# Values of the first six pairs of heads multiplied in plain float32, and the first token mix at two units per slot

## The chip, the cores and the metric

The kernel runs on one core of a Trainium2 chip. The metric is the device time of one execution in microseconds; lower is better. TensorE (PE) multiplies, VectorE (DVE), ScalarE (ACT) and GpSimd (POOL) work on what it leaves, and the queue of SyncE (SP) starts the transfers.

## What is computed

Decay attention over 8 batches of 8 heads (576 tokens, head size 64), and then a token mix of low rank and a feed-forward layer, all in float32:

```python
scores = q @ k.T / sqrt(D) + cum[:, None] - cum[None, :]   # cum: cumulative log of f, causal
attn = softmax(scores)
x = concat_heads(attn @ v)                                 # [8, 576, 512]
u = x + (x.T @ U @ V).T                                    # U, V of rank 32
out = u + relu(u @ w_ch1) @ w_ch2                          # 512 -> 2048 -> 512
```

The weights arrive as 64-bit floats and are decoded on the chip.

## The kernel before

**Split operands.** A product in float32r takes one array pass but keeps fewer bits of its operands. So the kernel splits an operand into a high part (`h`, a rounding copy on ACT) and a low part (`l`, the rest, a subtraction on DVE or POOL) and adds several products. For the values, `make_vs` lays the high and the low part of V side by side in the 128 columns of the stationary operand `VS`, one arrangement per head; `evac` brings the transposed probabilities from PSUM as `PTh` (ACT, line 380) and `PTl` (DVE, line 381); `values` multiplies `VS` with `PTh` and then with `PTl` (lines 462 and 465), so that the two halves of the result `pv` hold the products with high V and with low V. ACT copies one half out (`cr`, line 473) and DVE adds the other (`xT`, line 474).

**Steps and slots.** The program goes through 32 pairs of heads. Step `p` has ten slots `s`. In step `p` PE scores pair `p` (head 0 in slots 0 to 3, the tails of both heads in 4 and 5, head 1 in 6 to 9), transposes the probabilities of pair `p-1` (`T`, `T_v`), multiplies the values of pair `p-1`, head 0 (slot 7) and of pair `p-2`, head 1 (slot 0), transposes the results (`Tx`, `Ty`) and projects them on the rank (`ranks`, `Tt`). PE's order is the order of the code. That of DVE, ACT and POOL is set by a scheduler, and in steps 1 to 6 that of SP's queue too. `defer` and `at` write the work of the other engines into later slots.

**Operands of the scores.** `split_qk` makes the parts of q and k (`HL`), and `place` copies them by DMA into `G[0]` and `G[1]`, one per head of a pair, each a single buffer: the next pair's parts can go there when the last score of this head is done.

**Decodes.** Fourteen weight blocks are decoded by `decode` (four operations on DVE, lines 61 to 64, three on POOL, one on ACT). Two come at the start, and the table `DECODES` gives step and slot of the other twelve, the last six of which are blocks of the second weight matrix.

**Fillers.** After the fourth pair of a batch has gone through, ten mix units of that batch (five `hmix`, five transposes `tu`, `tv`) are taken one per slot of a step; for the first batch this is step 6. Then its feed-forward units (24 or 27 per batch, `A` of twelve 256-column products, `B` of six 512-column products) fill slots 1 to 6, 8 and 9 of the next steps. Four are held back for the slots of the next mix. Mix units and feed-forward units share the two PSUM banks of the pool `psF`. The stores of the mixed tokens to DRAM (`ud`) follow the last mix unit.

**After step 33** a second sweep goes over the rest of the hidden features, batch by batch.

Of the kernel before, what the change touches and what calls it, by code (L numbers as in the profile page):

```python
# [8 lines left out]
F32 = mybir.dt.float32  # L9
F32R = mybir.dt.float32r  # L10
# [7 lines left out]
B, H, S, D = 8, 8, 576, 64  # L18
# [15 lines left out]
PTW = 1536  # L34
NG = B + 1
NX = 3


@with_exitstack
def tile_decay_attention_moe(ctx, tc, qk, v, f, U, V, w1, w2, out):  # L40
# [9 lines left out]
    def decode(raw, a, h, l, eng, rows=slice(0, 128), keep=False):  # L50
        """float64 words (low, high) of `raw` [.., 2] as float32 in two parts h + l [..]; `a`
        is int32 scratch, and so is `raw` in the end. Read as a float32, the high word has the
        sign and the upper bits of the exponent in the right place: a product changes the bias.
        `eng`: the engine for a part that several can do; `rows`: where the low part is wanted;
        `keep`: not before what `eng` has been given so far."""
        lo, hi = raw[..., 0].bitcast(U32), raw[..., 1]
        af, gf = a.bitcast(F32), hi.bitcast(F32)
        first = eng.tensor_scalar(af, gf, 2.0**-112, None, op0=ALU.mult)
        if keep:
            tc.keep_in_program_order(first)  # L60
        nc.vector.tensor_scalar(hi, hi, -0x80000000, None, op0=ALU.bitwise_and)
        nc.vector.scalar_tensor_tensor(a, a, 3, hi, op0=ALU.logical_shift_left, op1=ALU.bitwise_or)
        nc.vector.tensor_scalar(hi, a, -0x800000, None, op0=ALU.bitwise_and)
        nc.vector.scalar_tensor_tensor(gf, lo, 2.0**-52, gf, op0=ALU.mult, op1=ALU.mult)
        nc.gpsimd.tensor_tensor(af, af, gf, op=ALU.add)
        nc.scalar.copy(h, af)
        nc.gpsimd.tensor_tensor(l[rows], af[rows], h.bitcast(F32)[rows], op=ALU.subtract)
# [23 lines left out]

# [1 line left out]
    DG, ZR = 384, 512  # L93
    HW = S // 2
    # Operands of the scores, per head of a pair: planes 0, 1 hold q (stationary), 2, 3 hold k.
    # Columns: head 0 [main 512 | tail 64 | zeros 64], head 1 [zeros 64 | tail 64 | main 512]
    # (k of head 1 keeps its order).
    G = [att.tile([P, 4, 640], F32R, name=f"G{j}") for j in range(2)]
# [30 lines left out]

# [1 line left out]
    def decay_log():  # L131
# [24 lines left out]

# [1 line left out]
    w1h = wt.tile([P, NA, NDC, P], F32R, name="w1h")  # L158
# [3 lines left out]
    Us = wt.tile([P, NM + 1, 2 * RK], F32R, name="Us")  # L162
    VV = wt.tile([P, S], F32R, name="VV")  # rows: the high part three times, the low part once

# [12 lines left out]

    # The decodes, in order: each takes its turn in the tiles that the first sweep uses later.
    UNITS = [("w1", 0), ("w1", 1), ("U", 0), ("w1", 2), ("w1", 3), ("V", 0), ("w1", 4), ("w1", 5)]
# [3 lines left out]
    def load_w(u):  # L183
# [4 lines left out]
        if kind == "w2":  # L188
            # The last buffer of X has no use before batch 2.
            spare = xn[NX - 1].rearrange("p c d -> p (c d)").bitcast(I32)  # L190
            if fc % 2:
                raw, a = spare[:, 1536:2560], sb.tile([P, 512], I32, tag="w2a", name=f"stg{u}")
            else:
                raw, a = spare[:, 0:1024], spare[:, 1024:1536]
        else:
            t = sf.tile([P, 3 * S], I32, tag=("uh", "ul", "hh")[u % 3], name=f"stg{u}")
            raw, a = t[:, 0 : 2 * n], t[:, 2 * n : 3 * n]
# [32 lines left out]

# [1 line left out]
    st = {}  # L232
    filler = []
    SPARE = (2, 4)
    # Work of the other engines on what TensorE leaves behind, by slot and by phase in the slot.
    later = {}
# [21 lines left out]
    def load_v(p):  # L258
        vr = sb.tile([P, NM + 1, P], F32, tag="vr", name=f"vr{p}")
        st[p]["vr"] = vr.rearrange("p c (j d) -> p c j d", j=2)  # L260
# [3 lines left out]

    def make_vs(p):
        vr = st[p]["vr"]
        VS = sb.tile([P, NM + 1, 2, P], F32R, tag="VS", name=f"VS{p}")
# [7 lines left out]
    def split_qk(p, eng=nc.gpsimd):  # L275
        qk = st[p]["qk"]
        # Until the first sweep starts, one of its tiles serves as a second buffer.
        spare = p in SPARE
# [30 lines left out]
    def bank_s(p, name):  # L309
        """Before the first mix starts, the banks of the fillers serve the scores too."""  # L310
        scored[0] += 1
# [67 lines left out]
    def evac(dsth, dstl, src):  # L379
        defer(0, lambda: nc.scalar.copy(dsth, src))  # L380
        defer(2, lambda: nc.vector.tensor_tensor(dstl, src, dsth.bitcast(F32), op=ALU.subtract))  # L381

    GRP = (((0, 0), (0, 1), (0, 2), (0, 3)), ((1, 1), (1, 2), (1, 3)), ((2, 2), (2, 3), (3, 3)))

    def turn_p(p, j, g):
        z = st[p]
        if "PTh" not in z:
            z["PTh"] = sb.tile([P, 2, PTW], F32R, tag="PTh", name=f"PTh{p}")
# [12 lines left out]
        for c in sorted({c for c, _ in grp}):  # L401
            m = sum(1 for cc, _ in grp if cc == c)
            sl = slice(OC[c], OC[c] + P * m)
            evac(z["PTh"][:, j, sl], z["PTl"][:, j, sl], tp[:, P * x : P * (x + m)])
            x += m

    def turn_tail(p):
# [6 lines left out]
        for c in range(0, NM, 2):  # L414
            o = [(OC[c + y] + MAIN - P * (c + y)) // TAIL for y in range(2)]
            pair = [
                z[n].rearrange("p j (y d) -> p j y d", d=TAIL)[:, :, o[0] : o[1] + 1 : o[1] - o[0]]
                for n in ("PTh", "PTl")
            ]
            evac(pair[0], pair[1], tpv[:, :, c : c + 2])  # L420

    def turn_small(pa, px):
        """The last keys of pair pa's tail rows, and the last tokens of pair px."""
        tq = psT.tile([P, 512], F32, tag="T", name=f"Ty{pa}_{px}")
# [5 lines left out]
        if pa is not None:  # L430
            pt4 = st[pa]["PT4"]
            defer(0, lambda: nc.scalar.copy(pt4[0:64], tq[0:64, 0:P]))
            defer(
                2,
# [17 lines left out]
    X0 = 384  # L452

    def values(p, j):
        z = st[p]
        if j == 0:
# [47 lines left out]
    def ranks(p):  # L504
# [13 lines left out]

        # Rows of TS: the high parts of x Uh and x Ul, the low part of x Uh, its high part again.
        defer(1, lambda: nc.scalar.copy(TS[0:64, fs], tp[0:64, 0:P]))  # L520
# [7 lines left out]

# [1 line left out]
    cur = [None, None]  # L530

    def mix_units(b):
# [3 lines left out]
        def bank(name):  # L536
            # The banks of the scores are free when the last batch is mixed.
            if b == B - 1:
# [46 lines left out]
        if b < B - 1:  # L585
            return h + t
        # The first sweep of the last batch starts as soon as its first half is mixed.
        return h[0:2] + t[0:2] + h[2:] + t[2:]
# [109 lines left out]
    mixing = []  # L698
    DECODES = [(1, 1), (1, 3), (1, 6), (2, 2), (2, 6), (3, 3), (4, 2), (5, 2), (6, 1), (6, 4), (6, 7), (7, 1)]

    def step(p):
# [8 lines left out]
        for s in range(SLOTS if p <= NP else 6 + 2):  # L710
# [17 lines left out]
            if (p, s) in DECODES:  # L728
                u = 2 + DECODES.index((p, s))
                # The last four use a tile of X again, which the scheduler orders as written here.  # L730
                steps = [lambda: load_w(u + 2), lambda: decode_w(u)]
# [40 lines left out]
            if mixing:  # L772
                mixing.pop(0)[1]()
                if filler and (s in (0, 1, 3, 5) or p >= NP):
                    run_filler()
# [23 lines left out]

# [1 line left out]
    pool = pools(right, "right")  # L801
# [7 lines left out]
    def wb_unit(i, r):  # L809
# [4 lines left out]
        else:  # L814
            nc.sync.dma_start(t, w2_src(NA + i))
            h, l = b2h[i], b2l[i]
        # X of batch 5 is done with.
        a = xn[(B - 3) % NX][:, (2 * i + r) % NM].bitcast(I32)
# [22 lines left out]

# [1 line left out]
    pool = pools(left, "left")  # L843
# [9 lines left out]

    # The last batch comes first: its tokens and its partial sums are still on the chip.
    order = [B - 1, *range(B - 2), B, B - 2]
# [53 lines left out]
def _layout(q, k, v, f, moe_U, moe_V, moe_w_ch1, moe_w_ch2):  # L909
    """The inputs in the order the chip loads them: only rearranged, in their own types."""  # L910
    import numpy as np
# [38 lines left out]
```

## Time and profile before

| | |
|---|---|
| median of 3 runs | 1350.56 us (1349.6 to 1354.66) |
| profiled execution, first to last instruction | 1350.8 us |
| PE busy | 1245.0 us (92%) |
| DVE, ACT, POOL busy | 728.5, 559.8, 307.1 us |

The page shows the profiled execution by its span alone; this span stands for its own time. In the page's slices each digit is the busy share of a 33.8 us stretch in tenths. A table of stretches gives for each its length, the busy time of PE, of the weight loads (PEld), of DVE, ACT and POOL with the number of instructions, the clock that TensorE was granted, the busy share of the DMA engines and GB/s. A row of waits says which instruction waited for which, the sum in us, how often, and the longest.

### The profile page before, as it was taken

The page shows a single profiled execution, that of the slowest core. Times are in us where ns is not written, and L with a number is a line of the kernel's source. Part 1 is how long each engine was busy: PE and PEld are TensorE (multiplying, and loading weights), DVE is VectorE, ACT ScalarE, POOL GpSimd, SP SyncE. Part 2 cuts the span into 40 slices and gives each one's busy share as a digit, 9 for nine tenths or more (in the row PEclk, how much of TensorE's full clock was granted, in tenths as well). Part 3 has the DMA queues.
Part 4 walks back from the last instruction along what each step waited for, and adds up shares of the span by engine and source line. Part 5 has one row for each costly group of instructions (what it writes and reads, how often), then busy time and mean ns, then how long its engine had stood idle before and what let it go on. Part 6 is the DMA issues. An engine that isn't in the chain of part 4 may idle for free.

```text
span 1350.8 us, 19334 instructions
## 1 busy us (share of the span) xinstructions
PE 1245.0 (92%) x6912; PEld 1066.2 (79%) x6912; DVE 728.5 (54%) x1796; ACT 559.8 (41%) x1516; POOL 307.1 (23%) x228
## 2 busy tenths in 40 slices
PE   2678898999998998999999988999999999999998
PEld 2567787888887897888888877788888888888887
DVE  6797976767667667667667599621211212112121
ACT  4666766756666666667567322211101111011110
POOL 4675633222232322222131055400000000000000
PEclk9887899999999999999999999999999999999999
DMA  8966765754755656567544254410321303212010
GB/s 211 231 174 153 185 160 129 211 125 124 192 138 139 189 131 174 154 145 205 122 117 134 71 159 139 180 69 0 125 78 48 125 0 125 87 39 94 0 32 32
DMA packets 89431, 167.02 MB, mean 124 GB/s; under 512 B 8776, under 2 KB 33352, under 8 KB 87288
## 3 DMA queue, kind: packets, MB, share of 16 engines
q1 hardware_dynamic: 89336, 165.79, 44.5%
q8 instruction: 55, 0.90, 0.3%
q14 instruction: 40, 0.33, 0.1%
HBM read 73.33 MB, written 35.78 MB: 81 GB/s over the span
## 4 chain that ended last, share of the span: by engine, by line
PE 70%; DMA 10%; DVE 8%; ACT 5%; SPq 3%; issue 3%; POOL 0%; ACTq 0%; DVEq 0%; POOLq 0%
PE O L882 19%; PE Hb L870 18%; PE A L608 8%; DMA G<-HL 8%; PE B L626 6%; PE V L465 4%; PE S L304 3%; PE T L398 3%; PE S L305 2%; ACT HL L281 2%; PE Tt L515 1%; PE St L304 1%; PE St L305 1%; DMA G<-cumd 1%; SPq L289 1%
## 5 line engine op out<-in xcount | busy, mean ns | idle before, releaser
L875 DVE SCALAR_TENSOR_TENSOR bl<-Hb,bh 128x512 fp32r<-128x512 f32 x90 | 62.2, 692 | 377.6 <-ACT bh L874 377.6
L874 ACT ACTIVATE bh<-Hb 128x512 fp32r<-128x512 f32 x90 | 53.9, 599 | 429.3 <-PE Hb L870 429.3
L870 PE MATMUL Hb<-u,b1h 128*128 128x512 f32 x640 | 213.2, 396 | 0.0
L325 DVE CUSTOM_DVE_ANT_0 S<-S,mask 128x128 f32<-128x128 f32 (+3 forms) x256 | 126.3, 495 | 81.2 <-PE S L305 75.4
L333 ACT ACTIVATE P<-S,nm 128x128 f32<-128x128 f32 (+3 forms) x256 | 136.7, 535 | 63.7 <-DVE nm L325 56.5
L304 PE MATMUL S<-G 128*128 128x128 f32 (+3 forms) x256 | 98.4, 384 | 62.9 <-DMA G<-HL 31.2
L882 PE MATMUL O<-b2h,bl 128*128 128x512 f32 x360 | 142.8, 397 | 2.2 <-DVE bl L875 2.2
L870 PEld LDWEIGHTS Hb<-u,b1h 128*128 128x128 f32 x640 | 120.3, 188 | 29.2
L882 PE MATMUL O<-b2h,bh 128*128 128x512 f32 x360 | 142.2, 395 | 0.0
L882 PE MATMUL O<-b2l,bh 128*128 128x512 f32 x360 | 142.2, 395 | 0.0
L608 PE MATMUL A<-uh,w1h 128*128 128x256 f32 (+1 forms) x384 | 122.0, 318 | 5.6 <-DVE xn L636 4.1
L870 PE MATMUL Hb<-u,b1l 128*128 128x512 f32 x320 | 126.5, 395 | 0.0
L273 POOL TENSOR_TENSOR VS<-vr,VS 128x320 fp32r<-128x320 f32 x64 | 55.3, 884 | 299.8 <-PE T L398 211.3
L381 DVE TENSOR_TENSOR PTl<-T,PTh 128x512 fp32r<-128x512 f32 (+1 forms) x192 | 98.2, 532 | 36.2 <-ACT PTh L380 34.3
L304 PEld LDWEIGHTS S<-G 128*128 128x128 f32 x256 | 51.8, 202 | 81.1 <-ACT P L333 31.1
L608 PE MATMUL A<-uh,w1l 128*128 128x256 f32 (+1 forms) x384 | 114.6, 298 | 0.0
L608 PE MATMUL A<-ul,w1h 128*128 128x256 f32 (+1 forms) x384 | 114.4, 298 | 0.0
L626 PE MATMUL B<-w2h,hh 128*128 128x512 f32 x216 | 92.0, 426 | 4.6 <-DVE ost L644 2.5
L398 PE MATMUL T<-ident,P 128*128 128x128 f32 x544 | 92.0, 287 | 1.9 <-DVE xn L443 1.6
L282 POOL TENSOR_TENSOR HL<-qk,HL 128x1152 fp32r<-128x1152 f32 x30 | 79.7, 2656 | 50.9 <-ACT HL L281 46.5
L305 PE MATMUL S<-G 128*128 128x128 f32 (+3 forms) x256 | 86.7, 340 | 2.1 <-DMA G<-cm 2.1
L380 ACT CAST PTh<-T 128x512 fp32r<-128x512 f32 (+1 forms) x192 | 83.0, 462 | 11.3 <-PE T L398 9.4
(168 smaller groups left out, 2758.5 us busy)
## 6 DMA issues: line engine op xcount, KB each, us to landing
G<-HL SPq DMA_DIRECT2D x192, 288.0 KB
qk<-in_qk_dram SPq DMA_DIRECT2D x32, 576.0 KB
u<-ud SPq DMA_DIRECT2D x16, 1024.0 KB
sr<-in_w_dram SPq DMA_DIRECT2D x20, 512.0 KB
vr<-in_v_dram SPq DMA_DIRECT2D x32, 256.0 KB
accd<-ost SPq DMA_DIRECT2D x32, 256.0 KB
xn<-accd SPq DMA_DIRECT2D x8, 1024.0 KB
out_dram<-xn SPq DMA_DIRECT2D x32, 256.0 KB
```

What stands on the lines that cost most here:

```text
L282: eng.tensor_tensor(HL[:, :, 1], qk, HL.bitcast(F32)[:, :, 0], op=ALU.subtract)
L304: nc.tensor.matmul(ps, lhs[0], G[j][:, 2, cols], start=first, stop=False)
L305: nc.tensor.matmul(ps, lhs[1], G[j][:, 3, cols], start=False, stop=last)
L325: nc.vector.tensor_tensor_reduce(ps[:, :w], ps[:, :w], mask[:, 512 - w : 512], scale=-SCALE, scalar=3.0e38, op0=ALU.add, op1=ALU.min, accu ...
L333: nc.scalar.activation(pt, ps[:, :w], AF.Exp, bias=z["nm"][:, col : col + 1], scale=-1.0, accum_out=z["sm"][:, col : col + 1])
L380: defer(0, lambda: nc.scalar.copy(dsth, src))
L381: defer(2, lambda: nc.vector.tensor_tensor(dstl, src, dsth.bitcast(F32), op=ALU.subtract))
L398: nc.tensor.transpose(tp[:, P * x : P * x + P], z["P"][j][i][:, P * c : P * c + P], ident)
L608: nc.tensor.matmul(ps[:, :nt], wt[:, fc, c], ut[:, c, sl], start=m == 0, stop=m == 3 * NDC - 1)
L626: nc.tensor.matmul(ps, ht[:, fc, P * x : P * x + P], wt[:, fc], start=fc == 0 and m == 0, stop=fc == NA - 1 and m == 2,)
L870: nc.tensor.matmul(ps, wt_[i][:, c], ut[:, c, 0:MAIN], start=m == 0, stop=m == 3 * NDC - 1)
L882: nc.tensor.matmul(po[x], ht[:, P * x : P * x + P], wt_[i], start=i == 0 and m == 0, stop=i == NB - 1 and m == 2)
```

## The change

For the pairs 0 to 5 (`NF = 6`) V isn't split, and neither are the probabilities: `make_vs` does nothing, `evac` makes the high copy alone, now in plain float32, and `values_direct` multiplies V as it came with the probabilities, one set of five main products and one of 64 columns. Both heads of V are in the 128 stationary columns, so each head's result lies in its own half, and one DVE copy brings it out. `cr` and its ACT copy are gone for these pairs. The probabilities of odd pairs use the buffer of `PTl`, and V of odd pairs that of `VS`. In step 6 mix units go two a slot, so that they end in slot 4 and feed-forward units start in slot 5. In `DECODES` two slots are new, (4, 6) and (5, 6), and two are gone, (6, 7) and (7, 1).

```diff
+NF = 6
 def load_v(p):
-        vr = sb.tile([P, NM + 1, P], F32, tag="vr", name=f"vr{p}")
+        vr = sb.tile([P, NM + 1, P], F32, tag="VS" if p < NF and p % 2 else "vr", name=f"vr{p}")
 def make_vs(p):
+        if p < NF:
+            return
 def evac(dsth, dstl, src):
         defer(0, lambda: nc.scalar.copy(dsth, src))
+        if dstl is None:
+            return
         defer(2, lambda: nc.vector.tensor_tensor(dstl, src, dsth.bitcast(F32), op=ALU.subtract))
 def turn_p(p, j, g):
-        if "PTh" not in z:
+        if "PTh" not in z and p < NF:
+            z["PTh"] = sb.tile([P, 2, PTW], F32, tag=("PTh", "PTl")[p % 2], name=f"PTh{p}")
+            z["PT4"] = sb.tile([P, P], F32, tag="PT4", name=f"PT4{p}")
+        elif "PTh" not in z:
...
-            evac(z["PTh"][:, j, sl], z["PTl"][:, j, sl], tp[:, P * x : P * (x + m)])
+            evac(z["PTh"][:, j, sl], z["PTl"][:, j, sl] if p >= NF else None, tp[:, P * x : P * (x + m)])
+    def values_direct(p, j):
+        z = st[p]
+        if j == 0:
+            z["xT"] = sb.tile([P, S], F32, tag="xT", name=f"xT{p}")
+        vr, xT, pt = z["vr"].rearrange("p c j d -> p c (j d)"), z["xT"], z["PTh"]
+        pv = psV.tile([P, 1024], F32, tag="V", name=f"V{p}_{j}")
+        nc.tensor.matmul(pv[:, X0:512], vr[:, 0], pt[:, j, 0:P], start=True, stop=True)
+        for c in range(NM):
+            lo = max(P * c, P)
+            nc.tensor.matmul(
+                pv[:, X0 + lo : X0 + S], vr[:, c], pt[:, j, OC[c] + lo - P * c : OC[c] + S - P * c],
+                start=c == 0, stop=False,
+            )
+        nc.tensor.matmul(
+            pv[:, X0 + MAIN : X0 + S], vr[0:64, NM], z["PT4"][0:64, 64 * j : 64 * j + 64], start=False, stop=True
+        )
+        defer(1, lambda: nc.vector.tensor_copy(xT[OWN[j]], pv[OWN[j], X0 : X0 + S]))
 def values(p, j):
+        if p < NF:
+            values_direct(p, j)
+            return
-    DECODES = [(1, 1), (1, 3), (1, 6), (2, 2), (2, 6), (3, 3), (4, 2), (5, 2), (6, 1), (6, 4), (6, 7), (7, 1)]
+    DECODES = [(1, 1), (1, 3), (1, 6), (2, 2), (2, 6), (3, 3), (4, 2), (4, 6), (5, 2), (5, 6), (6, 1), (6, 4)]
             if mixing:
                 mixing.pop(0)[1]()
+                if mixing and p == NF:
+                    mixing.pop(0)[1]()
```

The tails and the last keys (`turn_tail`, `turn_small`) leave out their low parts in the same way.

On DVE, in step 4 around the first values of pair 3 (`S_1x` are scores of head 1 of pair 4, `V_0` is the values' bank, `T_1x` transposed probabilities, `xn_123` a weight block in decoding). Before:

```order
L381 TENSOR_TENSOR PTl_950<-T_10_1066,PTh_949 128x512
L381 TENSOR_TENSOR PTl_950<-T_11_1083,PTh_949 128x384
L325 ISA S_12_1108,nm_925<-S_12_1108,mask 128x384
L325 ISA nm_925 128x1
L474 TENSOR_TENSOR xT_1087<-V_0_1089,cr_1088 64x576
L381 TENSOR_TENSOR PTl_950<-T_12_1111,PTh_949 128x256
L381 TENSOR_TENSOR PTl_950<-T_12_1111,PTh_949 128x128
L61 TENSOR_SCALAR xn_123<-xn_123 128x512
L325 ISA S_13_1136,nm_925<-S_13_1136,mask 128x512
```

The same place now:

```order
L329 ISA S_11_986,nm_841<-S_11_986,mask 128x256
L329 ISA nm_841 128x1
L378 TENSOR_TENSOR sm_842<-sm_842 128x1
L483 COPY xT_993<-V_0_994 64x576
L329 ISA S_12_1006,nm_841<-S_12_1006,mask 128x384
L329 ISA nm_841 128x1
L329 ISA S_13_1032,nm_841<-S_13_1032,mask 128x512
```

The low parts are gone, and the result of the values is a copy that needs no ACT copy ahead of it.

On PE, at the start of step 6 (`H` are mix units; `V_1` the values of pair 4, head 1). Before:

```order
L462 MATMUL V_1_1366<-PTh_1163,VS_1219 128x128
L465 MATMUL V_1_1366<-PTh_1163,VS_1219 128x448 x2
L465 MATMUL V_1_1366<-PTh_1163,VS_1219 128x320
L465 MATMUL V_1_1366<-PTh_1163,VS_1219 128x192
L462 MATMUL V_1_1366<-PTl_1164,VS_1219 128x128
L465 MATMUL V_1_1366<-PTl_1164,VS_1219 128x448 x2
L465 MATMUL V_1_1366<-PTl_1164,VS_1219 128x320
L465 MATMUL V_1_1366<-PTl_1164,VS_1219 128x192
L469 MATMUL V_1_1366<-PT_1165,VS_1219 128x64
```

Now, up to the first score of slot 1:

```order
L473 MATMUL V_1_1241<-PTh_1054,vr_924 128x128
L476 MATMUL V_1_1241<-PTh_1054,vr_924 128x448 x2
L476 MATMUL V_1_1241<-PTh_1054,vr_924 128x320
L476 MATMUL V_1_1241<-PTh_1054,vr_924 128x192
L480 MATMUL V_1_1241<-PT_1055,vr_924 128x64
L407 MATMUL T_00_1250<-ident,P_00_1064 128x128
L407 MATMUL T_00_1250<-ident,P_01_1075 128x128
L407 MATMUL T_00_1250<-ident,P_02_1101 128x128
L407 MATMUL T_00_1250<-ident,P_03_1112 128x128
L579 MATMUL H_0_1255<-TS_633,VV 128x512
L579 MATMUL H_1_1257<-TS_633,VV 128x512
L308 MATMUL S_01_1274<-G_91 128x256
```

Five products stand where nine rows with the high and the low part stood, their stationary operand is V itself (`vr`), and two mix units follow in the slot.

On SP's queue, at the end of step 6 (`G_91` and `G_92` are the operands of heads 0 and 1, `HL_1462` the parts of q and k of pair 7, `ud` the stores of the first batch). Before:

```order
L256 DMA qk_1498<-in_qk_dram 128x1152
L289 DMA G_91<-HL_1462 64x2x576
L288 DMA G_91<-HL_1462 64x2x576
L290 DMA G_91<-HL_1462 64x2x576
L296 DMA G_91<-cumd 4x2x576
L202 DMA xn_123<-in_w_dram 128x1024
L288 DMA G_92<-HL_1462 64x2x576
L289 DMA G_92<-HL_1462 64x2x576
L290 DMA G_92<-HL_1462 64x2x576
L296 DMA G_92<-cumd 4x2x576
L576 DMA ud<-uh_1509 128x4x512
L576 DMA ud<-ul_1510 128x4x512
```

Now (`HL_1344` is pair 7):

```order
L265 DMA vr_1356<-in_v_dram 64x128 x2
L257 DMA qk_1389<-in_qk_dram 128x1152
L610 DMA ud<-uh_1305 128x4x512
L293 DMA G_91<-HL_1344 64x2x576
L610 DMA ud<-ul_1306 128x4x512
L292 DMA G_91<-HL_1344 64x2x576
L294 DMA G_91<-HL_1344 64x2x576
L300 DMA G_91<-cumd 4x2x576
L292 DMA G_92<-HL_1344 64x2x576
L293 DMA G_92<-HL_1344 64x2x576
L294 DMA G_92<-HL_1344 64x2x576
L300 DMA G_92<-cumd 4x2x576
```

The two stores stood behind both placements of pair 7; now one is ahead of the placement of its head 0 and one in the middle of it.

More of the change, by code (lines that the diff above doesn't have):

```diff
@@ L418, in turn_tail @@
                 for n in ("PTh", "PTl")
+                if n in z
             ]
-            evac(pair[0], pair[1], tpv[:, :, c : c + 2])
+            evac(pair[0], pair[1] if p >= NF else None, tpv[:, :, c : c + 2])
     def turn_small(pa, px):
@@ L432, in turn_small @@
             defer(0, lambda: nc.scalar.copy(pt4[0:64], tq[0:64, 0:P]))
-            defer(
+            if pa >= NF:
+              defer(
                 2,
```

## The prediction

> **What bounds the kernel now.** I read the page first, the busy shares and the slices, then a table of the first ten steps, then who waited for whom in them. A step is the ten slots of one pair of heads; I cut the steps where the first score product of a pair starts.
>
> ```profile
> span 1350.8 us, 19334 instructions
> PE 1245.0 (92%) x6912; PEld 1066.2 (79%) x6912; DVE 728.5 (54%) x1796; ACT 559.8 (41%) x1516; POOL 307.1 (23%) x228
> PE   2678898999998998999999988999999999999998
> ```
>
> PE carries the program: from the eighth slice on it is at 9 or 8 tenths. Only the first slices (33.8 us each) have room, and that is where the six pairs lie. The table (steps 1 to 7, 9 and 10; columns: length, then PE, PEld, DVE, ACT, POOL busy, granted clock, DMA share, GB/s):
>
> ```profile
> 32.20:54.15 21.95, 12.90 (x61) 11.62 (x61) 15.13 (x43) 13.10 (x38) 12.80 (x10) 0.95 0.90 230
> 54.15:73.96 19.81, 16.04 (x87) 14.14 (x87) 16.02 (x42) 12.37 (x38) 12.85 (x9) 0.79 0.91 226
> 73.96:94.09 20.13, 14.53 (x87) 12.91 (x86) 19.47 (x50) 14.11 (x41) 18.12 (x11) 0.83 0.72 189
> 94.09:112.47 18.38, 15.01 (x87) 12.75 (x86) 16.70 (x47) 13.54 (x43) 11.77 (x9) 0.81 0.63 146
> 112.47:133.19 20.72, 16.49 (x88) 13.82 (x86) 15.10 (x46) 13.62 (x40) 9.88 (x7) 0.75 0.63 157
> 133.19:159.18 25.99, 20.12 (x113) 17.24 (x112) 23.61 (x57) 16.45 (x47) 13.65 (x10) 0.80 0.59 144
> 159.18:182.92 23.74, 23.04 (x172) 21.50 (x172) 21.15 (x60) 17.42 (x50) 14.47 (x11) 1.00 0.76 207
> 206.41:225.76 19.35, 17.25 (x124) 15.58 (x123) 12.60 (x39) 13.43 (x41) 5.91 (x4) 1.00 0.61 142
> 225.76:249.50 23.74, 21.37 (x137) 17.95 (x137) 19.57 (x54) 16.04 (x46) 5.92 (x4) 1.00 0.56 138
> ```
>
> Steps 1 and 2 are bound by transfers (0.90 and 0.91 of the DMA engines). Steps 3 and 4 lean on DVE (19.47 of 20.13, 16.70 of 18.38). Step 5 has no engine near its length, but a clock of 0.75. Step 6 has DVE at 23.61 of 25.99. From step 7 on, filler units fill PE. The waits of PE in steps 3 to 5, and one stall with what it does to the clock:
>
> ```profile
> PE T_v L398 <- DVE xT L474: 4.5, 2, 2.7
> PE T_v L411 <- DVE PTl L381: 2.1, 1, 2.1
> PE St L304 <- ACT P L333: 1.5, 1, 1.5
> PE Tx L483 <- DVE PTl L381: 1.3, 2, 0.7
> ...
> PE V L462 <- DVE sm L374: 0.9, 1, 0.9
> ```
>
> ```profile
> 80.00:83.00 3.00, 2.98 (x12) 2.69 (x13) 2.91 (x8) 2.15 (x5) 2.51 (x3) 0.52 0.86 327
> 86.00:90.00 4.00, 3.27 (x15) 2.87 (x15) 3.96 (x13) 3.26 (x10) 4.00 (x3) 0.57 0.94 205
> 98.00:99.80 1.80, 0.01 (x1) 0.01 (x1) 1.74 (x7) 1.80 (x7) 1.14 (x2) 1.00 0.92 193
> 100.00:106.00 6.00, 5.26 (x22) 4.42 (x21) 5.06 (x15) 4.33 (x13) 5.84 (x5) 0.50 0.39 98
> ```
>
> DVE-caused waits in steps 3 to 5 are 4.5 + 2.1 + 1.3 + 0.9 = 8.8 us. After each of the longer ones PE runs at about half clock, as at 100.00, after 1.80 us without work.
>
> **What is taken away.** Six pairs lose the low parts of the probabilities (DVE), the copy of the second half of the result (ACT) and the split of V (ACT, POOL). What that was, in steps 1 to 6, one row each from three views, the line of the low parts, the tile of the copies and the tile of split V:
>
> ```profile
> 32.20:159.18 126.98, 25.93 (x58) 0.83 0.72 181
> 32.20:159.18 126.98, 8.30 (x11) 6.96 (x11) 0.83 0.72 181
> 32.20:159.18 126.98, 24.29 (x121) 22.54 (x121) 5.00 (x12) 10.48 (x12) 0.83 0.72 181
> ```
>
> So DVE loses 25.93 us, some 4.3 a step (the additions of 8.30 become copies of the same size, counted as equal); ACT loses 6.96 + 5.00 = 12.0, 2.0 a step; POOL 10.48. On DVE this reaches the end of a step only where DVE is waited for: 8.8 us in steps 3 to 5. In steps 1 and 2 it is covered by transfers; ACT there also stood still for V in front of other work:
>
> ```profile
> ACT VS L272 <- DMA vr<-in_v_dram: 6.1, 1, 6.1
> ```
>
> That wait goes, but scores wait for their operands by DMA in the same place. I take 1.0 us off steps 1 and 2 (ends: nothing, and 4.0, the tenth of 41.76 us that DMA leaves).
>
> **What is added: the unsplit product.** One head before, at full clock, from its first product to the next transpose, and at half clock; then units of twelve 256-column and six 512-column products:
>
> ```profile
> 74.13 0.28 PE L462 MATMUL V<-PTh,VS 128*128 128x128 f32 x1
> 74.24 0.86 PE L465 MATMUL V<-PTh,VS 128*128 128x448 f32 x4
> 74.94 0.24 PE L462 MATMUL V<-PTl,VS 128*128 128x128 f32 x1
> ...
> 75.77 0.66 PE L398 MATMUL T<-ident,P 128*128 128x128 f32 x4
> 128.22 0.46 PE L462 MATMUL V<-PTh,VS 128*128 128x128 f32 x1
> ...
> 131.02 0.42 PE L304 MATMUL S<-G 128*128 128x384 f32 x1
> 167.84 1.43 PE A L608 x12
> 191.34 1.39 PE B L626 x6
> ```
>
> A head takes 75.77 - 74.13 = 1.64 us for 3136 columns, 2.80 us at half clock. Unsplit it has 1600 columns. What a column of plain float32 costs no row shows. Lower end: the same as now, 1600 x 1.39 / (6 x 512) us = 0.72, 0.9 less than before. Upper end: the four part products that the split spells out (high and low probabilities, each against high and low V, which now share an array pass side by side; with both heads of V in the 128 columns they can't), one pass each at the rate of the first five products: 4 x (0.81 + 0.05) = 3.44, 1.8 more. I take four passes at the rate of wide products, 4 x 0.72 = 2.9, with 0.1 for short ones 3.0: 1.4 more a head, since the split kernel needs these four for the same accuracy. The Trainium skill, "FP8 and Floating Point Precision" (TensorE Precision Notes), also gives true FP32 four passes through the array; by it alone a head would cost 4 x 0.72 = 2.9 us, an estimate; no trace here shows it.
>
> **Steps 3 to 5.** Six heads add 6 x 1.4 = 8.4. The waits for DVE take 8.8 away: the result now goes to DVE in one copy, and a transpose bank is free after ACT's copy. Next late is ACT (1.5 at the tail scores, more in smaller rows), so I let nothing else go. The spells at half clock cost 3 x 0.48 + 4 x 0.43 + 6 x 0.50 = 6.2 us; half of them should not begin: -3.1. Sum 8.4 - 8.8 - 3.1 = -3.5. The two more decodes in the sixth slot of pairs 4 and 5 land on a DVE that has just lost 4.3 us a step, and are taken at nothing; without that cover each would cost its four DVE operations.
>
> **Step 6.** Mix units go two a slot, and four filler units move here from step 9, into the slots left. Step 10 has ten mix units and four fillers too, without the decodes: 23.74. With two unsplit heads, 23.74 + 2.8 = 26.5, against 25.99 now: +0.5. New waits: fillers and mix units share two banks, and with two units in a slot the second next one waits for DVE, one addition of this size each:
>
> ```profile
> L546 DVE TENSOR_TENSOR xn<-H,xn 128x512 f32<-128x512 f32 x4 | 2.7, 685 | 0.0
> ```
>
> Four such slots make 0 to 2.8 us; I add 0.5, because PE already idles 5.9 us of this step. Behind the waiting unit stand the next slot's scores. Step 6: +1.0.
>
> **Step 7.** One head (the second of pair 5) on a PE that is busy 23.04 of 23.74: +1.4. The first batch's two stores of mixed tokens come earlier, ahead of and between the placements of pair 7's operands on the queue (the order rows above). Rows: sizes, and the placement that the stores now precede; before they followed the second one:
>
> ```profile
> ud<-uh SPq DMA_DIRECT2D x7, 1024.0 KB
> 146.55 0.65 SPq L289 DMA_DIRECT2D G<-HL  x1
> 162.32 1.34 SPq L576 DMA_DIRECT2D ud<-uh  x1
> ```
>
> 2.1 MB at 230 GB/s is 9.1 us, the placement's 0.9 MB 3.9: 13.0 us, where 159.18 - 146.55 = 12.6 are left: 0 to 2 us, I take 0.5. Step 7: +1.9.
>
> **Step 9** loses its four units: PE falls to 17.25 - 4 x 1.4 = 11.6 and no longer sets the length. The nearest step without units is step 4, 18.38, with a decode in it; the floor is ACT's 13.43. I take 17.5, near the first: -1.9. Step 8 and everything from step 10 on, where fillers are level again, stay.
>
> Sum: -1.0 - 3.5 + 1.0 + 1.9 - 1.9 = -3.5 against 1350.8, so 1347.3; the median of the runs shown is 0.2 below that span: **1347**. A measurement can tell about 0.5% (6.8 us) here, so this is no change.
>
> **Rivals.**
> - *The clock comes back.* The unsplit products keep the array busy for nearly twice as long at a stretch, no long stall is left in steps 3 to 5, and they shrink to the length of step 9 less its four units plus two heads, 19.35 - 5.6 + 2.8 = 16.6, at best; at 17.3 each that is -7.3, with -3.0 in steps 1 and 2, -1.5 in step 6, +1.4 in step 7, -3.0 in step 9: 1337. For it: clock 1.00 in steps 7 to 10. Against: step 5's spell begins after ACT waits, which stay. The Trainium skill, "TensorE: Matmul & The Clock Gate" (Part 1), lets sustained matmul activity release the throttle, and takes about 3.4 us without work to bring it back; the direction agrees with the rows at 98.00 and 100.00, the threshold does not, since 1.80 us were enough.
> - *Slower: the new products run at half clock.* They stand behind the same short stalls, so nine heads of steps 3 to 7 take 2 x 3.0 instead of 2.80, 3.2 more each and not 1.4, and the regained clock (3.1) is lost: -3.5 + 16.2 + 3.1, that is 1366 with all, 1357 to 1360 with half of them. For it: clock 0.75 to 0.83 in steps 3 to 6. From 2.5 us more a head on these nine it is slower by over 0.5%.
> - *New waits in steps 6 and 7.* Bank waits at their 2.8 and stores that hold pair 7 up by 4 us: 1353. For it: the order; against: slack in both places.
> - *Nothing moves the end*, since transfers pace these steps: 1350. For it: share 0.90 in steps 1, 2; against: 0.63 to 0.72 in 3 to 5. I count this within the forecast.
>
> **How the numbers follow.** Forecast 0.48, with 1341 to 1354 of its own (head price 0.9 less to 1.8 more, covered in part): of this 0.10 faster, 0.36 same, 0.02 slower. Clock 0.25, all faster. Half clock 0.17, all slower. New waits 0.10, half same, half slower. Together 0.35, 0.41, 0.24. The range reaches from a little under the clock case, 1334, to the middle of the half-clock case, 1361.
>
> **What would show it.** Right: no waits for xT or PTl in steps 1 to 6; a head's unsplit products from first to next instruction about 3.0 us at full clock; DVE under 17 us in steps 3 to 5, which together take about 55.7; step 6 near 27, step 9 near 17.5, equal lengths from step 10. Wrong: a head under 2 us or over 4; a clock of 1.00 through steps 3 to 6; scores of pair 7 waiting for DMA by more than 2 us.

## The result, and the profile after

The changed kernel takes 1366.34 us (median of 4 runs, 1365.11 to 1368.3), the kernel before beside it 1352.24 (1349.6 to 1354.66): a ratio of 1.0096, 95% interval 1.0072 to 1.012. It is 14 us slower; 1347 was forecast, with 1361 as the upper end. The profiled execution took 1365.77 us, its span 1364.0.

The lines of the page of after that answer to those shown of before:

```profile
span 1364.0 us, 19227 instructions
PE 1259.3 (92%) x6924; PEld 1065.8 (78%) x6924; DVE 705.8 (52%) x1730; ACT 549.6 (40%) x1492; POOL 294.8 (22%) x216
PE   2788898999998999999999988999999999999998
```

DVE, ACT and POOL have less to do, and PE has 14.3 us more. The totals do not tell where the time is lost. The table by steps does (steps 1 to 7, 9 and 10, cut as in the prediction; columns as there):

```profile
32.34:54.10 21.76, 14.04 (x61) 11.54 (x62) 12.66 (x33) 11.89 (x35) 11.96 (x9) 0.86 0.99 243
54.10:73.95 19.85, 17.31 (x88) 12.38 (x89) 11.20 (x33) 11.57 (x36) 11.52 (x8) 0.89 0.85 210
73.95:93.33 19.38, 16.58 (x88) 12.23 (x89) 17.64 (x38) 11.29 (x33) 14.12 (x10) 0.91 0.76 197
93.33:110.89 17.56, 14.67 (x89) 11.01 (x88) 12.06 (x37) 11.81 (x40) 9.28 (x7) 1.00 0.65 153
110.89:132.24 21.35, 16.45 (x88) 12.46 (x89) 14.89 (x41) 12.77 (x37) 12.59 (x8) 0.92 0.70 173
132.24:165.74 33.50, 27.31 (x162) 22.65 (x162) 22.21 (x54) 17.39 (x47) 15.60 (x11) 0.90 0.58 163
165.74:193.21 27.47, 25.69 (x150) 21.84 (x149) 14.62 (x44) 13.66 (x42) 5.86 (x4) 0.94 0.46 110
216.79:235.36 18.57, 13.69 (x88) 11.46 (x86) 11.48 (x36) 12.63 (x38) 5.86 (x4) 0.91 0.63 148
235.36:259.02 23.66, 21.24 (x136) 17.81 (x136) 19.27 (x54) 15.87 (x46) 5.92 (x4) 1.00 0.56 138
```

Up to the start of step 6 the two kernels are level (132.24 against 133.19). Step 6 takes 33.50 us instead of 25.99: PE's busy time in it rises by 7.2 us, and its idle time stays (6.2 us, before 5.9). Step 7 takes 27.47 instead of 23.74, step 9 18.57 instead of 19.35. At the start of step 11 the changed kernel is 9.65 us behind (259.02 against 249.37; the last row shown of before ends at the second product there, 249.50). The rest of the difference comes in this execution from two short spells near 450 and 550 us. The first, as a table of two stretches, has PE waiting beside full DMA engines and then a low clock:

```profile
450.00:454.00 4.00, 2.25 (x20) 2.02 (x18) 1.59 (x4) 1.92 (x5) 0.93 (x2) 1.00 1.01 342
454.00:458.00 4.00, 4.00 (x19) 3.76 (x20) 2.59 (x7) 2.27 (x8) 2.20 (x1) 0.57 0.99 321
```

Step 6, PE's waits (sum, times, longest), and then its timeline in the middle of the step (start, duration, engine, line, operation, what out of what, and in brackets the idle time ahead of it and what ended it):

```profile
PE S L308 <- ACT P L337: 2.8, 2, 2.2
PE Tv L602 <- DVE ul L584: 2.6, 1, 2.6
PE Tu L593 <- DVE ul L584: 1.3, 1, 1.3
```

```profile
140.59 0.69 PE L308 MATMUL S<-G 128*128 128x384 f32 x1 [2.20 <-ACT P L337]
...
146.35 0.63 PE L593 MATMUL Tu<-ident,xn 128*128 128x128 f32 x4 [1.32 <-DVE ul L584]
...
147.55 0.60 PE L593 MATMUL Tu<-ident,xn 128*128 128x128 f32 x4
150.73 0.66 PE L602 MATMUL Tv<-ident,xn 64*128 64x64 f32 x4 [2.57 <-DVE ul L584]
```

The transposed mixed tokens (`Tu`, `Tv`) use two banks, and a bank is free when DVE has made the low part `ul`. On DVE the `ul` for which `Tv` waits stands behind an operation of a weight decode, and the clock of TensorE falls behind the stall (DVE's timeline, and a table of two stretches, during the stall and after it):

```profile
148.36 1.62 DVE L63 SCALAR_TENSOR_TENSOR stg<-stg,xn 128x512 int32<-128x512 int32 x1
149.90 0.68 DVE L584 TENSOR_TENSOR ul<-Tu,uh 128x512 fp32r<-128x512 f32 x1
```

```profile
148.50:150.70 2.20, 0.00 (x0) 0.00 (x1) 2.20 (x4) 0.89 (x2) 1.47 (x2) 0.98 0.44 169
150.70:155.00 4.30, 4.27 (x24) 4.17 (x25) 2.48 (x7) 2.47 (x8) 3.38 (x3) 0.62 0.82 231
```

The first wait, that of a score for ACT, and the long one of ACT in step 7 have one cause: the cast of the next pair's operands (`HL`) stands on ACT ahead of the first exponentials of the step and waits until a placement by DMA has left its buffer. On ACT in step 6, before and now, the cast and the first exponential (`P`) of head 0:

```profile
137.22 0.36 ACT L333 ACTIVATE P<-S,nm 128x128 f32<-128x128 f32 x1
139.91 1.15 ACT L281 CAST HL<-qk 128x1152 fp32r<-128x1152 f32 x1 [1.76 <-POOL VS L273]
```

```profile
139.03 1.15 ACT L285 CAST HL<-qk 128x1152 fp32r<-128x1152 f32 x1 [3.48 <-DMA G<-HL]
140.08 0.36 ACT L337 ACTIVATE P<-S,nm 128x128 f32<-128x128 f32 x1
```

And at the start of step 7 now (the row names no releaser for the cast; the placement of head 1 of pair 7, asked for from 164.5 us on, is what it waited for):

```profile
171.16 1.15 ACT L285 CAST HL<-qk 128x1152 fp32r<-128x1152 f32 x1 [4.69 <-issue]
172.93 0.36 ACT L337 ACTIVATE P<-S,nm 128x128 f32<-128x128 f32 x1
```

### The profile page after: what moved, and what is told of

Same layout as the page of the kernel before. It is cut to its first block, busy times and chain, and to the rows that moved or that the text cites. A ratio compares the mean times of both kernels' runs of the same rounds, so it can differ in the third digit from the quotient of the medians.

```text
span 1364.0 us, 19227 instructions
## 1 busy us (share of the span) xinstructions
PE 1259.3 (92%) x6924; PEld 1065.8 (78%) x6924; DVE 705.8 (52%) x1730; ACT 549.6 (40%) x1492; POOL 294.8 (22%) x216
## 4 chain that ended last, share of the span: by engine, by line
PE 70%; DMA 10%; DVE 7%; ACT 5%; SPq 4%; issue 3%; POOL 0%; ACTq 0%; DVEq 0%; POOLq 0%
PE O L918 19%; PE Hb L906 18%; PE A L642 8%; DMA G<-HL 7%; PE B L660 6%; PE V L499 3%; PE S L308 3%; PE T L407 3%; DMA G<-cumd 2%; PE S L309 2%; ACT HL L285 2%; PE Tt L549 2%; PE St L308 1%; PE St L309 1%; DVE xn L63 1%
## 5 line engine op out<-in xcount | busy, mean ns | idle before, releaser
L277 POOL TENSOR_TENSOR VS<-vr,VS 128x320 fp32r<-128x320 f32 x52 | 44.6, 878 | 290.8 <-PE T L407 217.1
L387 DVE TENSOR_TENSOR PTl<-T,PTh 128x512 fp32r<-128x512 f32 (+1 forms) x156 | 79.8, 532 | 40.4 <-ACT PTh L384 39.1
L660 PE MATMUL B<-w2l,hh 128*128 128x512 f32 x216 | 85.6, 396 | 0.0
```

Of the source, the lines that this page charges most:

```text
L660: nc.tensor.matmul(ps, ht[:, fc, P * x : P * x + P], wt[:, fc], start=fc == 0 and m == 0, stop=fc == NA - 1 and m == 2,)
```

## The experiments

The three parts of the change were first taken singly, then step 6 was taken apart, then the price of the unsplit product. Times are medians; ratios are to the kernel before, run beside. Executions of one kernel spread by some 5 us to each side, so steps are compared as well as totals; each step length is from one execution. Steps differ less from one execution to the next, but not always: steps 3 to 5 together took 58.3 to 60.9 us in the changed kernel and five variants of it whose edits concern only later steps.

**Without the paired mix units** (the changed kernel otherwise).

```diff
-                if mixing and p == NF:
-                    mixing.pop(0)[1]()
```

> The change with one part undone: the first token mix runs one unit per slot again (the six unsplit pairs and the new decode slots stay). Theory M (the two mix units per slot and what they pull forward cost the time: bank waits of mix units on DVE, the first batch's stores ahead of pair 7's operands): steps 6 and 7 fall from 33.5 and 27.5 us to about 27.5 and 25, step 9 rises by about 1, the whole is about 1355. Theory P (the price of the unsplit products on PE costs it, wherever PE has no idle time): step 6 and 7 keep their length less the four units moved, the whole stays at 1363 to 1366.

1356.37 us, ratio 1.0018 (1.0002 to 1.0035); step 6 took 26.57 us, step 7 24.86, about as theory M had it. Against the kernel before, run beside each, the loss falls from 14.1 us to 2.5: put on top of the other two parts, the second mix unit in a slot costs 11.6 us.

**The mix and the decodes without unsplit products.**

```diff
-NF = 6
+NF = 0
-                if mixing and p == NF:
+                if mixing and p == 6:
```

> One part alone: values split as before in all pairs, but two mix units per slot in step 6 and the new decode slots. Theory M: about 1361, with stalls of mix units on DVE and of ACT on the operands of pair 8 as in the change. Theory P: 1351 to 1354, as before.

1360.74 us, ratio 1.0054 (1.0036 to 1.0072), as theory M had it. This is 6.9 us behind before; with the unsplit products on top it is 14.1, so they cost 7.2 there. What a part costs depends on which others are in place. Its profiled execution has a span of 2405 us, so its steps are not compared.

**Only the new slots for decodes.**

```diff
-NF = 6
+NF = 0
-                if mixing and p == NF:
-                    mixing.pop(0)[1]()
```

> One part alone: values split, one mix unit per slot, only the new decode slots. Theories M and P: 1350 to 1355, no change. Theory D (the two decodes that come earlier load DVE in steps 4 and 5, where it has least room): 1358 or more, with steps 4 and 5 longer by 3 us together.

1357.59 us, ratio 1.0023 (1.0009 to 1.0036). The profiled execution has a span of 1351.5, and its steps 8 to 13 start within 0.2 us of where those of before do. It is the shortest of its twelve executions. Steps 4 and 5, where theory D looked, took 37.4 us in it, 39.1 before. Where the 3.7 us of the median are lost is not shown.

**Only the unsplit products.**

```diff
-                if mixing and p == NF:
-                    mixing.pop(0)[1]()
-    DECODES = [..., (4, 2), (4, 6), (5, 2), (5, 6), (6, 1), (6, 4)]
+    DECODES = [..., (4, 2), (5, 2), (6, 1), (6, 4), (6, 7), (7, 1)]
```

> Only the unsplit products of six pairs: one mix unit a slot, the decodes in the slots that they had before. If the higher price of a head (3.0 us for 1.6, 12 heads, 16.8 us) is paid in full by the waits for DVE that go and by the clock, the whole is 1352 to 1356 and step 6 about 26; if the old slots of the decodes alone explain the rest of what the run with one mix unit a slot loses to the kernel before, it is 1350 to 1353; if the unsplit products are a net loss, 1358 or more.

1360.76 us, ratio 1.0055 (1.0034 to 1.0077), 5.0 us behind by step 11. A net loss by themselves; with the new slots for decodes (the first run) they are 1.5 us behind by step 11.

**Only the paired mix units.** The diff of the second run, and that of `DECODES` of the run just above:

```diff
-NF = 6
+NF = 0
-                if mixing and p == NF:
+                if mixing and p == 6:
-    DECODES = [..., (4, 2), (4, 6), (5, 2), (5, 6), (6, 1), (6, 4)]
+    DECODES = [..., (4, 2), (5, 2), (6, 1), (6, 4), (6, 7), (7, 1)]
```

> Only the mix at two units a slot in step 6: values split for all pairs, decodes in the slots that they had before. If the paired units cost by themselves what they cost in the changed kernel (waits for DVE and the half clock behind them): step 6 at 31 to 34 us, the whole at 1360 to 1364. If they cost it only beside unsplit heads, whose products take 4.2 us and not 3.0 when the clock is at half: step 6 at 28 or less, the whole at 1354 to 1358.

1370.76 us, ratio 1.0133 (1.0102 to 1.0164), the slowest of all, and slower than either theory had it, though step 6 is as the first one said. Its steps 6 and 7:

```profile
134.63:168.01 33.38, 26.25 (x160) 22.75 (x160) 27.10 (x69) 19.48 (x55) 16.30 (x12) 0.85 0.70 188
168.01:196.72 28.71, 26.18 (x146) 22.92 (x147) 18.85 (x48) 13.99 (x41) 10.87 (x9) 0.88 0.37 93
```

So the pairing does not need unsplit heads to cost. And the parts do not add up: singly they lose 6.3, 3.7 and 16.3 us, together 14.1. That the unsplit products relieve DVE, for which the paired units wait, does not show in step 6: it is as long here as in the changed kernel (33.38 and 33.50 us), and PE waits as long for DVE (3.7 and 3.9 us), though DVE is busy for 27.10 us here, with a third decode, and for 22.21 there. This run loses its further time ahead of step 6 (2.4 us) and in steps 7 and 9 (1.2 and 1.8).

**Feed-forward units kept out of step 6.** The mix still runs two units a slot.

```diff
-            if not mixing and pending:
+            if not mixing and pending and p != NF:
```

> The changed kernel, but the first feed-forward units begin in step 7 as before, though the mix still runs two units a slot. Theory A (what costs is that four feed-forward units were moved into step 6, where PE had no room for them: its busy time there rose by 5.9 us over the run with one mix unit a slot, 27.31 against 21.39, and the idle time did not fall): step 6 back to 26 to 27.5 us, step 9 to 19.4, the whole at 1355 to 1359. Theory B (two mix units in a slot wait for banks and for DVE, whatever comes behind them): step 6 stays at 31 or more, the whole at 1362 or more.

1362.54 us, ratio 1.007 (1.0048 to 1.0093). Step 6 still took 32.63 us though 5.7 us of products had left it. Theory A fell for this step. Two stretches of it:

```profile
152.00:156.00 4.00, 2.77 (x13) 2.37 (x12) 1.98 (x7) 2.15 (x9) 2.52 (x3) 0.50 0.79 216
156.00:160.00 4.00, 4.00 (x11) 2.48 (x10) 0.49 (x2) 1.85 (x5) 1.27 (x1) 0.50 0.99 269
```

The clock stays at half for 8 us behind the waits; in the changed kernel it is at half up to 154.0 us and at 1.00 behind that, with PE busy. The four units moved into step 6 fill idle time, and cost 0.9 us there. But they cost more behind it: without them the cast on ACT stands behind the first exponential in step 7, which takes 24.62 us instead of 27.47, and by step 11 this run is 3.0 us ahead of the changed kernel.

**No decode in step 6.**

```diff
-    DECODES = [..., (3, 3), (4, 2), (4, 6), (5, 2), (5, 6), (6, 1), (6, 4)]
+    DECODES = [..., (3, 3), (3, 7), (4, 2), (4, 6), (5, 1), (5, 4), (5, 7)]
```

> The changed kernel with no weight decode in step 6: its two decodes take slots of pairs 3 and 5 instead. Theory C (the two decodes on DVE hold up the low parts of the mixed tokens, for which PE waits): step 6 at 29.5 us or less, steps 3 to 5 at most 2 us longer, the whole at 1361 to 1363. Theory A (PE's own work sets the length of step 6): step 6 at 32 to 33.5, the whole at 1364 to 1367.

1362.13 us, ratio 1.0073 (1.0046 to 1.0099). Step 6 took 31.73 us, between the theories: the wait of `Tv` fell from 2.6 to 0.6, but a mix unit now waited 2.5 for its addition on DVE. The total is in the range of theory C, though steps 3 to 5 took 61.4 us, 3.1 more than in the changed kernel. The decode is one of several things in the way, not the cause.

**Low parts of the first batch's mixed tokens made on GpSimd, as zeros,** so that ACT alone frees the banks; what is left out is their true value.

```diff
+            if b == 0:
+                defer(1, lambda: nc.gpsimd.tensor_scalar(dl, dh.bitcast(F32), 0.0, None, op0=ALU.mult), 2)
+                return
```

> The changed kernel, but the low parts of the first batch's mixed tokens are left out: GpSimd writes zeros in their place from the high parts, so that DVE has no part in freeing the banks of the transposed tokens. If PE's waits for those low parts (1.3 and 2.6 us in step 6) and the half clock after them set step 6: these waits go, step 6 at 26.5 to 28.5 us, the whole at 1356 to 1360. If other waits of the same slots take their place (ACT for the scores, the additions of the mix on DVE): step 6 at 31 or more, the whole at 1363 to 1367.

1359.09 us, ratio 1.0052 (1.0033 to 1.007). Step 6, its row and PE's waits in it:

```profile
133.65:162.03 28.38, 25.98 (x162) 21.45 (x163) 19.61 (x49) 16.78 (x47) 22.68 (x16) 0.94 0.69 194
```

```profile
PE S L308 <- ACT P L337: 2.5, 2, 1.9
PE S L308 <- ACT Ptl L366: 0.4, 1, 0.4
```

Both waits for `ul` are gone, 3.9 us, and the step is 5.1 shorter. That DVE makes `ul` late is shown to be a cause; as the run also takes these subtractions off DVE (19.61 us busy, not 22.21), it doesn't tell the bank from the load.

**The cast of pairs 7 and 8 kept in order on ACT.**

```diff
-        nc.scalar.copy(HL[:, :, 0], qk)
+        (tc.keep_in_program_order if p in (7, 8) else id)(nc.scalar.copy(HL[:, :, 0], qk))
```

> The changed kernel, with the cast of the operands of pairs 7 and 8 kept on ACT behind the work that was written before it. In the changed kernel that cast stands ahead of the first exponentials of steps 6 and 7 and waits there for a placement by DMA (3.5 and 4.7 us). If this is what makes step 7 longer: step 7 from 27.5 to about 24.5, the scores' wait for ACT in step 6 (2.8) under 1, the whole at 1360 to 1363. If the placement itself is what is late: step 7 at 26.5 to 27.5, the whole at 1364 to 1367.

1360.29 us, ratio 1.0043 (1.0023 to 1.0064). Steps 6 and 7:

```profile
135.92:165.60 29.68, 24.72 (x162) 20.03 (x162) 23.04 (x54) 17.81 (x49) 15.55 (x11) 1.00 0.74 197
165.60:189.54 23.94, 23.94 (x148) 20.48 (x148) 14.72 (x44) 13.08 (x39) 5.92 (x4) 1.00 0.42 109
```

Step 7 lost 3.5 us and is back to the 23.74 of before within 0.2; step 6 lost 3.8, with a granted clock of 1.00 in both. So the order of this cast is a second cause of step 6's length and the main one of step 7's. In step 6 it is not a matter of PE's waits alone: those for ACT fell by 2.2 us and those for `ul` from 3.9 to 2.5, but one of 2.2 for the placement came up at its end. The other 2.6 us are busy time, at a clock of 1.00 instead of 0.90. The two causes overlap: the run above gave 5.1 us back, this one 3.8, together more than the 7.5 lost, and no run takes both away.

**The stores of the first batch behind both placements of pair 7.**

```diff
-            defer(4, use, 2)
+            defer(4, use, 2 if b else 8)
```

> The change with one suspected cost taken away: the first batch's stores of mixed tokens are issued six slots later, behind both placements of pair 7. Theory M, the part on the stores: ACT's stall of 4.7 us early in step 7 goes, step 7 falls from 27.5 to about 24, the whole is about 1362. If the stall comes from the order on ACT alone, step 7 stays at 27 and the whole at 1366. Theory P: 1366.

1365.41 us, ratio 1.0079 (1.0056 to 1.0101). Step 7 took 25.82 us, 1.65 less, but this is not shown to be the stores' doing. The stall of the cast on ACT stayed (4.6), PE's wait behind it too (1.7 us, now 1.8), and what differs is the granted clock, 1.00 against 0.94. Two runs above whose stores stay early, the one without decodes in step 6 and the one with zeros, have step 7 at 25.85 and 25.88 us, at 1.00 as well. And step 9 took 1.8 us more here, at 0.83. So the stores are not shown to cost anything. This execution has no late spell of low clock, but is 12.2 us behind before from step 10 on.

**Unsplit products in pairs 8 to 13** instead of 0 to 5; one mix unit a slot, decodes as before. In all places that ask for the pair:

```diff
+F32P = range(8, 14)
-        if p < NF:
+        if p in F32P:
```

> The unsplit products in pairs 8 to 13 instead of 0 to 5, where PE is at 9 tenths and filler units stand in every step; the mix one unit a slot, the decodes as before. If the price of a head is covered only by the room that PE has in steps 3 to 6: 12 x 1.4 = 16.8 us longer less a few us of waits, 1364 to 1371, ratio 1.008 to 1.013. If relief on DVE and ACT pays for it everywhere: ratio within 1.003, 1350 to 1357.

1370.53 us, ratio 1.0132 (1.0102 to 1.0162). The kernel is level with before at the start of step 8 (-0.3) and 14.5 us behind at the start of step 17: 14.8 / 12 = 1.2 us a head where PE is full, of the 1.4 by which a head is longer. This is an average: step 12 alone is 5.9 us longer, with a wait of 2.2 us for ACT and a clock of 0.95.

**Most of the unsplit products left out** (one mix unit a slot, new slots for decodes; of the main products only that of the first token block is made, 640 columns a head with the others, so the values are incomplete).

```diff
                 start=c == 0, stop=False,
             )
+            break
```

> One mix unit a slot and the new slots for decodes, unsplit products in pairs 0 to 5, of which all but the first token block's and the tail's are left out: 640 columns a head and not 1600, by the 3.0 us of the whole head about 1.2 us, 1.8 less for each of 12 heads. If the price of the unsplit product is what sets steps 3 to 5 (59.0 us with it): they fall by 6 x 1.8 = 10.8 to 48, steps 6 and 7 by 1.8 to 5.4, the whole at 1337 to 1342. If other waits hold these steps (scores for ACT, operands by DMA, DVE's own work): steps 3 to 5 at 55 or more, the whole at 1347 to 1354.

1356.62 us, ratio 1.0025 (0.9998 to 1.0052). Steps 3 to 5, here and then in the first run of this section, with whole products:

```profile
74.05:94.69 20.64, 13.99 (x77) 11.30 (x76) 17.12 (x41) 12.52 (x39) 13.42 (x9) 0.78 0.79 185
94.69:113.58 18.89, 15.31 (x77) 11.74 (x76) 13.94 (x34) 11.53 (x37) 12.13 (x9) 0.79 0.59 141
113.58:135.57 21.99, 13.38 (x77) 10.18 (x76) 13.54 (x40) 12.70 (x39) 10.99 (x8) 0.92 0.71 163
```

```profile
73.85:93.59 19.74, 15.67 (x89) 11.25 (x88) 18.31 (x39) 11.53 (x35) 14.89 (x10) 1.00 0.75 193
93.59:111.56 17.97, 14.87 (x90) 11.08 (x88) 12.47 (x37) 11.79 (x40) 9.82 (x8) 1.00 0.65 150
111.56:132.84 21.28, 16.61 (x88) 12.46 (x88) 15.13 (x41) 12.74 (x37) 12.58 (x8) 0.92 0.69 172
```

At full clock a head takes 1.5 us here, a little more than expected, and 1.6 less than a whole one. Without these 6 x 1.6 = 9.6 us of products the three steps take 61.5 us and not 59.0: PE's products do not set their length. In step 3 of these two executions GpSimd does: with short products PE reaches the products that need its low part `xl` (`Tt`) earlier and waits for it longer, until about the same time. Here, and then in the first run:

```profile
92.33 0.37 PE L550 MATMUL Tt<-xl,Us 128*64 128x128 f32 x1 [4.83 <-POOL xl L171]
```

```profile
92.19 0.28 PE L549 MATMUL Tt<-xl,Us 128*64 128x128 f32 x1 [0.59 <-POOL xl L171]
```

In step 4 PE waits for `xT` on DVE (2.6 us, in the first run 2.4), in step 5 for ACT (6.0 and 4.0). Only step 6 (23.05, not 26.57) and step 7 (24.18, not 24.86) became shorter; the total is above what either theory had.

**The cast in order in the kernel before,** and **with one mix unit a slot in the changed one.**

> The kernel before, with the cast of the operands of pairs 7 and 8 kept on ACT behind the work that was written before it; nothing else is changed. If the cast holds up the scores in the kernel before too (2.6 us of waits for ACT in step 6): step 6 at 23 to 24.5 us instead of 25.99, the whole 1.5 to 3 us shorter, ratio 0.998 to 0.999. If another wait takes its place (operands of pair 8 placed later, DVE at 23.6 of 26 us): step 6 at 25.5 to 27, ratio 1.000 to 1.002.

> The changed kernel with one mix unit a slot, and the cast of the operands of pairs 7 and 8 kept in order on ACT. Without the latter step 6 took 26.57 us and step 7 24.86, with 3.8 us of waits of the scores for ACT in step 6. If those go: step 6 at 23.5 to 25, step 7 at 23.7 to 24.3, the whole 2 to 4 us shorter than without, ratio to the kernel before 0.998 to 1.000. If the wait only moves (to the placement by DMA): step 6 at 26 or more, ratio 1.001 to 1.004.

1356.88 us, ratio 1.0015 (0.9997 to 1.0034), and 1355.03, ratio 1.0006 (0.9986 to 1.0026). Steps 6 and 7 of the first:

```profile
132.91:153.82 20.91, 16.08 (x111) 13.17 (x111) 18.70 (x51) 15.78 (x44) 11.62 (x8) 1.00 0.63 154
153.82:182.21 28.39, 23.93 (x173) 21.52 (x171) 25.87 (x62) 17.43 (x50) 16.19 (x12) 1.00 0.69 190
```

Step 6 fell by 5.1 us, more than expected, and step 7 took 4.7 of it back: DVE, with the decodes, is next late there (25.87 of 28.39; PE waits 4.4 us for it, 0.7 before). In the second, step 6 fell to 22.26 and step 7 rose to 25.90; the two together are 3.3 us shorter than without the ordered cast, and the total shows no more than its spread. No version is faster than the kernel before by a margin that these runs can tell.

## Why the prediction was wrong

**The price of a head was right.** At the start of step 7 of after one head goes from its first product to the next transpose in 169.00 - 165.91 = 3.09 us (3.0 was taken):

```profile
165.91 0.44 PE L473 MATMUL V<-PTh,vr 128*128 128x128 f32 x2
166.18 2.53 PE L476 MATMUL V<-PTh,vr 128*128 128x448 f32 x8
168.64 0.43 PE L480 MATMUL V<-PT,vr 64*128 64x64 f32 x2
169.00 0.66 PE L407 MATMUL T<-ident,P 128*128 128x128 f32 x4
```

Five main products show as 2 and 8 records, two for each. The time is near four times 0.72 us, so it agrees with four passes, which the Trainium skill gives in "FP8 and Floating Point Precision" (TensorE Precision Notes).

**Steps 1 and 2** lost 0.15 us instead of 1.0: PE waits there for the operands of the scores by DMA, 8.8 us in all, 9.0 before.

**Steps 3 to 5** took 58.29 us, where 55.7 was forecast and 59.23 stood before. The step that failed is the sum "8.4 - 8.8 - 3.1". It added a price and two gains as if each reached the end. The run with short products shows that the 8.4 does not reach it: taking even more away doesn't shorten the steps. The 8.8 did not go either: the waits for `PTl` did, but 2.4 of 4.5 us for `xT` stayed, one of 2.0 for DVE's `xn` came up, and ACT and DMA came next:

```profile
PE S L308 <- ACT P L337: 3.0, 2, 2.7
PE T_v L407 <- DVE xT L483: 2.4, 1, 2.4
PE T L407 <- DVE xn L454: 2.0, 1, 2.0
PE S L308 <- DMA G<-HL: 1.5, 2, 1.0
```

The clock did come back (0.91 to 1.00, before 0.75 to 0.83), but the steps became only 0.9 us shorter. The longer products fill idle time, which may be what kept the clock up; it is not shown by itself, since the run with short products (0.78 to 0.92) also had longer waits between them.

**Step 6** is the main error: +7.5 us, where +1.0 was forecast. The term "four such slots make 0 to 2.8 us; I add 0.5" priced one addition on DVE per pair of units. PE's idle time of 5.9 us, on which this counted, was not filled: it stayed at 6.2, though PE was busy for 7.2 us more. The additions (`H`) were not waited for in the changed kernel. The transposed units were, because their banks need two engines, ACT and then DVE, and on DVE the low parts stand behind decodes and masks: 3.9 us of waits for two units, and a lower clock behind the stalls. The estimate also held step 10 to be a model for step 6; step 10 spreads its mix units over ten slots. And it had no term for the cast on ACT. In step 6 of before it stands behind the first exponential; now it stands ahead of it, as in the run with unsplit products alone. In step 7 none of the parts alone has it ahead of that exponential; the changed kernel as a whole has (171.16 and 172.93). Taking away the one cause gave 5.1 us back, the other 3.8; the two overlap. And the kernel before gains 5.1 us in step 6 from the ordered cast too, so its length there already held a price of the cast. That the change brought a loss to step 6 is shown for the second mix unit and the waits for `ul`; how much of it the cast adds stays open.

**Step 7** was forecast at +1.9 and came at +3.7. The cast on ACT is the whole of it (with it in order the step is 23.94): a wait of 1.8 us, and a spell of low clock behind it that three other runs with the same wait don't have and that is worth some 1.6. The terms of the forecast, 1.4 for the head and 0.5 for the stores, are not what was paid: PE waited for no placement here, and nothing shows a price of the stores. **Step 9** fell by 0.8 and not 1.9: PE, busy for 13.69 us, waited 4.8 for ACT (2.1 before), and the clock was 0.91 instead of 1.00. Steps 8 and 10 stayed (23.58 and 23.66), as forecast.

**The rivals.** "New waits in steps 6 and 7" came nearest to the mechanism, with a chance of 0.10, at 1353: it had bank waits and a pair 7 that comes late, but waits for the additions and the stores, not for the low parts and the cast, and no lost clock. "The new products run at half clock" gave 1366, the measured number, by luck, for a reason that did not hold: the clock rose in steps 3 to 5, and five of the six heads there took 3.0 to 3.1 us, the sixth 4.1. Why the profiled execution lost 4 us more near 450 and 550 us stays open: the run with late stores has no such spells, and its span is only 1.1 us shorter.

## What to carry to other kernels

Before adding a price to a gain in one stretch, ask whether either reaches the end of that stretch: here 9.6 us of products could be taken out of three steps without shortening them, while in another place, where PE was full, the longer products cost 1.2 us a head on average. When units are paired, price each by every engine that must touch its bank before it is free, and by what stands ahead of it there, and count the clock lost behind a stall as well as the stall. Removing work from an engine can let its scheduler pull a blocked instruction forward: look in the new order for instructions that wait for a transfer ahead of those on the path.

## What was not expected of the hardware

More work on PE can cost nothing in a stretch that something else sets, and here it went with a higher clock. In steps 3 to 5 the granted clock was 0.78 to 0.92 with short products and 0.92 to 1.00 with whole ones, in steps of nearly the same length. Step 6, with the same mix, took 32.63 us without the four feed-forward units and 33.50 with them, 5.7 us of products at full clock. One stall of 2.57 us was followed by 4.3 us at 0.62. But the same stall need not bring the clock down each time: behind the wait of 1.7 to 1.8 us in step 7 the clock fell in the changed kernel (0.94 over the step) and stayed at 1.00 in three runs with the same wait. The Trainium skill, "TensorE: Matmul & The Clock Gate" (Part 1), has the direction, that activity releases the throttle; its span without work of about 3.4 us is longer than either stall.
